# LSH attention and a mixture of causal heads: the second pair of heads without a scale, and one ring for q and k

## The chip, the cores and the metric

One core of a Trainium2 chip. The metric is the device time of one launch in microseconds; lower is better. TensorE (PE) does matmuls and transposes, VectorE (DVE), ScalarE (ACT) and GpSimd (POOL) elementwise work and reductions; in this kernel SyncE (SP) issues every DMA.

## The reference

Two stages, for 4 sequences (B) of 768 rows (S). The first is attention in 8 heads (H) of 64 columns (D) in which a query sees only the keys of its own bucket; the bucket is the sign pattern of 6 projections:

```python
q_bits = (einsum('bhsd,dk->bhsk', q, proj) > 0)          # same for k
mask = q_bucket[:, :, :, None] == k_bucket[:, :, None, :]
scores = where(mask, scale * q @ k.T, -1e9)               # scale = 1/8
x = softmax(scores) @ v                                   # heads side by side: (B, S, 512)
```

The second is a mixture of 4 causal heads (E) on x, of which a row takes the two with the largest gate logits:

```python
q, k, v = x @ wq[e], x @ wk[e], x @ wv[e]
ye = softmax(causal(scale * q @ k.T)) @ v @ wo[e]
out += (row chose e) * weight * ye
```

Inputs and output are 32-bit floats.

## The kernel before

**Units.** The work is cut into 48 units of attention: 32 of the first stage (`("L", b, h)`, written L0 to L7 here for the first sequence) and 16 of the second (`("M", b, e)`). `seq` is their order; the first sequence's L0 to L7 come first, later the mixture's units of sequence b − 1 stand between the heads of sequence b. Step i of the main loop is unit `seq[i]`. Heads are prepared in pairs (`hp`); the first pair is L0 and L1, the second L2 and L3, the third L4 and L5.

**One unit of the first stage.** Scores are made twice. `max_steps` (tile `mx`) makes them with queries on partitions, and DVE reduces their row maxima into `pm` (or `pmw` for a wide unit); `shift_steps` turns these into a row that is moved by DMA into the q operand (`qa<-row`, or `xth<-roww`). Then `s_unit` makes the transposed scores in 9 chunks of 512 (tile `st`, each from two products, `ka` with `qa` and `kb` with `qb`), ACT takes the exponential of each chunk twice (`p32` in four bytes, shown as p; `ph` in two), POOL makes the remainder `pl`, and PE multiplies with `vh` and `vl` into `o` (`av`). The maxima of `seq[i + 2]` are listed at step i. Bucket signs are extra rows of the operands, made in `signs`: `m0` on DVE, `M` (or `Mw`) on ACT, then four moves by DMA (`move`).

**Two widths.** A product of 32-bit precision is built from a rounded value and a remainder. Narrow operands are two-byte floats, and so that nothing leaves their range, q, k and v of a pair are scaled by powers of two from their largest absolute values: `pair_scales` reduces natq, natk and natv on DVE (tile `mqk`, 128x768) and goes through two matmuls' worth of transposes and some ten small DVE operations (`scale_of`) to `CS`. `prep_pair` then transposes q and k (PE), writes the scaled value (`qa`, `ka`) and the remainder (`qb`, `kb`), and projects for the signs with `pbh` and `pbl`, which `proj_halves` makes from proj. Wide operands are four-byte (`float32r`) and need no scale: `prep_first` does so for the first pair alone, in buffers of the names `xth` and `xtl` that later hold the mixture's input; it writes a plain copy as well (`T`), which the projection `pbd` reads in four bytes. Its v is scaled by itself in `prep_v`. Either way the halves of the operands lie on the wrong partitions at first and are moved by DMA (in the prep functions, and in `halves`).

**Buffers.** Narrow operands have four rings of `QB` = 5 buffers ("qa", "ka", "qb", "kb"), for units of both stages (`prep_pair`, `proj_steps`). A ring gives its buffers in the order in which they are asked for.

**Order.** All instructions are first recorded, each with the operations that it depends on. A `gate` adds a dependence that the data don't have (for example, the load of the second pair's q waits for the first pair's last remainder, `marks["t"]`, that of k for the signs, `marks["m"]`). `Recorder.schedule` then plans all engines with a cost for each operation: an engine takes what can start first, and among those what was recorded first. The plan sets the order of each engine's queue; on the chip each works through its queue in order. Background work is a list of jobs with a first and a last step (`job(first, last, generator, needs...)`). Until the first `av` PE runs placeholder matmuls (`o<-ident`) where it would be idle.

All operations are issued in one helper, so the profile shows line L423 for all of them; they are told apart by their tiles.

Of the kernel before, what the change touches and what calls it, by code (L numbers as in the profile page):

```python
# [429 lines left out]
LN_SHIFT = 5.545177444479562  # L430
EPS = 1e-9 * 256.0
LAG = 4
QB = 5
SCT = 4.0
FILL_GAP = 40.0
COLD = 4500.0
C0 = C1 = C2 = C3 = C4 = C5 = C6 = C7 = C8 = 0.0
FIRST = {("k", 1): "m", ("v", 1): "row", ("q", 2): "m", ("k", 2): "m"}
P1 = -3
YB = 2  # L440
NATB = 2
GS = "t"
W0 = 2
WN = 1
RATE = 750.0
# [4 lines left out]
def tile_kernel(ctx, tc, q, k, v, proj, w_gate, wq, wk, wv, wo, out):  # L450
# [20 lines left out]
    def raw(ap):  # L471
        return ap.bitcast(FT)
# [6 lines left out]

    def load(nm, src, b, hp):  # L480

        nc.gate = marks[FIRST.get((nm, hp), "m" if nm == "v" else "t") if not b else "m" if nm == "v" else "t"]
# [182 lines left out]

    def pair_scales(b, hp):

        second = (b, hp) == (0, 1)
        while second and "t" not in marks:
            yield 0  # L670
        m = sb.tile([128, 3], FT, name="mqk", bufs=2)
        names = "qk" if second else "qkv"
        for i, nm in enumerate(names):
            nc.gate = marks[GS] if second else None
            nc.vector.tensor_reduce(m[:, i:i + 1], NAT[nm, b, hp].rearrange("p h j d -> p (h j d)"), axis=AX.X, op=OP.max,
                                    apply_absolute_value=True)
            nc.gate = None
# [12 lines left out]
        yield 330  # L690
# [8 lines left out]
            a, n = (ds[g % 2]["qa"], MR) if g < 2 else (ds[g % 2]["ka"], MR + rows)  # L699
            move(a[D:D + n].rearrange("p (j s) -> p j s", j=2), M[32 * g:32 * g + 2 * n][:, None, :])  # L700

    def prep_first():

        ds = []
        lo, hi = slice(0, D), slice(D, 2 * D)
        ev, od = slice(0, HS), slice(HS, S)
        for h in range(2):
            d = U["L", 0, h] = dict(wide=True)
            d.update({n: sb.tile([128, S], FR, name=t, bufs=4) for n, t in
                      (("qa", "xth"), ("ka", "xtl"), ("qb", "xth"), ("kb", "xtl"))})  # L710
            ds.append(d)
        nats = {nm: NAT.pop((nm, 0, 0)) for nm in "qk"}
        TT = {nm: sb.tile([128, 2, HS], FT, name="T" + nm, bufs=1) for nm in "qk"}
        M = sb.tile([128, HS], FR, name="Mw", bufs=1)
        for nm, h in [("q", 0), ("k", 0), ("q", 1), ("k", 1)]:
            d, nat, T = ds[h], nats[nm], TT[nm]
            a, r = (d["qa"], d["qb"][:, od]) if nm == "q" else (d["ka"], d["kb"][:, ev])
            p = misc()
            for t in range(NT // 2):
                nc.tensor.transpose(p[:, t * 128:(t + 1) * 128],  # L720
                                    nat[:, h, 2 * t:2 * t + 2].rearrange("p j d -> p (j d)"), ident)
            nc.copy(T[:, h], p[:, :HS], bias=C0)
            nc.copy(a[:, ev], p[:, :HS], 0.125 if nm == "q" else None, bias=C0)
            if nm == "q":
                marks["t"] = nc.vector.scalar_tensor_tensor(r, p[:, :HS], 0.125, raw(a[:, ev]), op0=OP.mult,
                                                            op1=OP.subtract)
            else:
                marks["t"] = nc.vector.tensor_tensor(r, p[:, :HS], raw(a[:, ev]), op=OP.subtract)
            nc.sync.dma_start(raw(a[lo, od]), raw(a[hi, ev]))
            if nm == "k":  # L730
                p = misc()
                gs = (h, 2 + h)
                for g in gs:
                    nc.tensor.matmul(p[32 * g:32 * g + 32, :HS], pbd, TT["q" if g < 2 else "k"][:, h], start=True,
                                     stop=True, tile_position=(0, 32 * g))
                signs(p, gs, ds, [slice(32 * g, 32 * g + 32) for g in gs], M, 2, 1)
            yield 109 * (NT // 2)
        marks["m", 0, 0] = marks["m"]
        yield 700

    def proj_halves():
# [16 lines left out]
    def prep_pair(b, hp):  # L758
# [2 lines left out]
        lo, hi = slice(0, D), slice(D, 2 * D)  # L761
        ev, od = slice(0, HS), slice(HS, S)
        for h in range(2):
            d = U["L", b, 2 * hp + h] = {}
            d.update({n: sb.tile([128, S], HF, name=n, bufs=QB) for n in ("qa", "ka", "qb", "kb")})
            ds.append(d)
        nats = {nm: NAT.pop((nm, b, hp)) for nm in "qk"}
        c = SC.pop((b, hp))
        parts = []
# [359 lines left out]
        yield 0  # L1129

    def proj_steps(b, e):
        qa, ka, qb, kb = (sb.tile([128, S], HF, name=n, bufs=QB) for n in ("qa", "ka", "qb", "kb"))
        if b not in QKC:

            sc = QKC[b] = sb.tile([128, 4], FT, name="qkc")
# [128 lines left out]
    for b in range(B):  # L1264
        for hp in range(HP):
            i = pos["L", b, 2 * hp]
            if b or hp:
                loads.append((i - 4.5 if b or hp > 1 else P1, "q", q, b, hp))
                loads.append((i - 4.5 if b or hp > 1 else P1, "k", k, b, hp))
            loads.append((i - 4.5 if b or hp > 1 else P1 if not hp else -1, "v", v, b, hp))  # L1270
            job(max(i - 3.4, -1) if b or hp else -5, max(i - 2.6, -0.5) if b or hp else -4, prep_pair(b, hp) if b or hp else prep_first(),
                *([("sc", b, hp), "pb"] if b or hp else []))
            if not (b or hp):
                job(-1.3, -1, proj_halves())
            if b or hp:
# [142 lines left out]
```

## Time and profile before

| | |
|---|---|
| three timed runs | 671.19, 672.34, 673.12 us; median 672.34 |
| the profiled execution | 673.69 us, its span 671.9 us |
| mean granted TensorE clock | 0.996 |
| busy share of the span | PE 96%, PE weight loads 77%, DVE 76%, ACT 75%, POOL 70% |
| DMA | 50.02 MB, mean 74 GB/s |

The span is the time from the first to the last instruction. A busy PE is not PE at its peak: matmuls are pipelined, and their ends are modelled. What a stage is worth is read from that stage, so the rows below cut the span into stages.

### The profile page before, as it was taken

Reading aid. Unit: us, or ns where it says so; the run is one execution under the profiler, and the core shown is the slowest. Engines: PE = TensorE matmul, PEld = TensorE weight load, DVE = VectorE, ACT = ScalarE, POOL = GpSimd, SP = SyncE. Lnnn points to the kernel's source line nnn. Section 1 sums busy time; section 2 is a strip of 40 time slices with the busy share of each in tenths; the row PEclk is TensorE's granted clock in tenths of the full one; section 3 lists DMA queues with packets and bytes.
Section 4 is the critical chain, followed back from the end, with each engine's and each line's share of the span. In section 5 each row is a group of like instructions: output and inputs, shape, how many; then the busy total and the mean of one; then the engine's idle time right before and its main releaser. Section 6 shows DMA issues by size and latency. Waiting matters only on the chain.

```text
span 671.9 us, 21643 instructions
## 1 busy us (share of the span) xinstructions
PE 647.9 (96%) x8344; PEld 515.9 (77%) x8344; DVE 511.2 (76%) x1281; ACT 505.4 (75%) x1081; POOL 467.9 (70%) x496
## 2 busy tenths in 40 slices
PE   8998898999999999999999999899999999999997
PEld 7876666667887787888778777688778778789885
DVE  5969799898779786976975797886985867456652
ACT  3286888987887978876975879695995687953773
POOL 3186889887786968775883788584795596961652
PEclk9998999999999999999999999999999999999999
DMA  4642634444042334233132333323142221011222
GB/s 102 126 97 58 137 76 98 111 86 114 14 106 59 80 73 96 49 74 76 43 85 81 96 93 65 86 55 78 26 100 68 81 65 32 3 26 28 58 83 96
DMA packets 109933, 50.02 MB, mean 74 GB/s; under 512 B 88446, under 2 KB 106246, under 8 KB 109830
## 3 DMA queue, kind: packets, MB, share of 16 engines
q1 hardware_dynamic: 109830, 48.64, 30.7%
q8 instruction: 66, 1.08, 0.7%
q14 instruction: 37, 0.30, 0.2%
HBM read 20.98 MB, written 6.29 MB: 41 GB/s over the span
## 4 chain that ended last, share of the span: by engine, by line
PE 75%; DVE 11%; DMA 6%; ACT 3%; SPq 2%; issue 2%; POOL 1%; POOLq 0%; ACTq 0%; DVEq 0%
PE misc L423 27%; PE st L423 20%; PE o L423 19%; PE mx L423 10%; DVE pm L423 5%; DMA natv<-in_v_dram 3%; SPq L423 2%; ACT ph L423 1%; POOL pl L423 1%; ACT p L423 1%; DVE mqk L423 1%; DMA ka<-M 1%; DVE misc L423 1%; DMA qb<-qb 1%; DMA kb<-kb 1%
## 5 line engine op out<-in xcount | busy, mean ns | idle before, releaser
L423 POOL TENSOR_TENSOR pl<-p,ph 128x512 f16<-128x512 f32 (+2 forms) x384 | 423.9, 1130 | 184.6 <-ACT ph L423 107.3
L423 ACT ACTIVATE p<-st 128x512 f32<-128x512 f32 (+2 forms) x386 | 232.6, 603 | 52.3 <-PE st L423 49.8
L423 DVE TENSOR_REDUCE pm<-mx 128x2 f32<-128x512 f32 (+3 forms) x398 | 239.7, 621 | 30.6 <-PE mx L423 28.8
L423 ACT ACTIVATE ph<-st 128x512 f16<-128x512 f32 (+2 forms) x384 | 229.4, 602 | 1.2 <-PE o L423 1.2
L423 PEld LDWEIGHTS <-ph 128*128 128x128 f16 x2976 | 154.4, 98 | 24.7 <-issue 4.0
L423 PE MATMUL st<-qa,ka 78*128 78x512 f16 (+1 forms) x488 | 153.0, 323 | 3.0 <-ACT ph L423 1.6
L423 PE MATMUL st<-qb,kb 128*128 128x512 f16 x488 | 151.3, 321 | 0.0
L423 PEld LDWEIGHTS <-pl 128*128 128x128 f16 x1488 | 136.0, 97 | 9.3 <-POOL pl L423 4.3
L423 PE MATMUL mx<-ka,qa 76*128 76x512 f16 (+1 forms) x488 | 133.8, 322 | 5.1 <-DVE pm L423 2.4
L423 PE MATMUL o<-vh,pl 128*128 128x65 f16 x1152 | 126.1, 193 | 1.6 <-POOL pl L423 1.6
L423 PE MATMUL o<-vh,ph 128*128 128x65 f16 x1152 | 126.4, 194 | 0.7 <-DVE xp L423 0.2
L423 PE MATMUL o<-vl,ph 128*128 128x64 f16 x1152 | 126.1, 192 | 0.3 <-POOL vl L423 0.3
L423 PEld LDWEIGHTS <-qa 76*128 76x128 f16 (+1 forms) x488 | 44.9, 98 | 26.9 <-issue 9.3
L423 PEld LDWEIGHTS <-kb 128*128 128x128 f16 x488 | 48.1, 98 | 19.4 <-issue 5.2
L423 PEld LDWEIGHTS <-ka 78*128 78x128 f16 (+1 forms) x488 | 47.8, 98 | 14.7 <-issue 4.0
L423 PEld LDWEIGHTS <-ident 128*128 128x128 bf16 x469 | 36.7, 102 | 14.0 <-issue 4.8
L423 PE MATMUL o<-mvh,pl 128*128 128x65 f16 x336 | 35.8, 194 | 0.0
L423 PE MATMUL o<-mvh,ph 128*128 128x65 f16 x336 | 35.7, 194 | 0.0
L423 PE MATMUL o<-mvl,ph 128*128 128x64 f16 x336 | 35.7, 192 | 0.0
L423 PE MATMUL misc<-xth,wqk_h 128*128 128x384 f32 x128 | 32.1, 367 | 0.1
L423 DVE SCALAR_TENSOR_TENSOR kb<-misc,qkc,qa 128x384 f16<-128x384 f32 x32 | 19.6, 611 | 15.2 <-ACT qa L423 13.2
L423 POOL TENSOR_TENSOR vl<-cv,vh 128x384 f16<-128x384 f32 x32 | 28.2, 887 | 4.0 <-ACT vh L423 3.9
(204 smaller groups left out, 1126.5 us busy)
## 6 DMA issues: line engine op xcount, KB each, us to landing
natv<-in_v_dram SPq DMA_DIRECT2D x16, 384.0 KB
natq<-in_q_dram SPq DMA_DIRECT2D x15, 384.0 KB
natk<-in_k_dram SPq DMA_DIRECT2D x15, 384.0 KB
out_dram<-ot SPq DMA_DIRECT2D x20, 256.0 KB
qb<-qa SPq DMA_DIRECT2D x46, 96.0 KB
kb<-ka SPq DMA_DIRECT2D x46, 96.0 KB
ka<-qa SPq DMA_DIRECT2D x16, 96.0 KB
qb<-kb SPq DMA_DIRECT2D x16, 96.0 KB
```

The lines of the kernel that those rows point to most:

```text
L423: getattr(getattr(self.nc, e), m)(*[real(x) for x in args], **{k: real(x) for k, x in kw.items()})
```

## The change

The second pair of the first sequence is prepared as the first one: `prep_first` becomes `prep_wide(hp)`, for pairs 0 and 1.

- `pair_scales` is no longer called for the second pair: no mqk of q and k, no scale. Its preparation asks for the load of k and the end of the first pair's (`("pw", 0)`), not for the scale and the projection's halves.
- The load of its q is gated by nothing (`FIRST`), and the job runs from step −1.5 (`J1`), with a gate at the last projection of the pair before (`marks["p"]`).
- For the second pair the order is q, q, k, k, and the projections of both heads are made at the end, their signs with one operation on 128 partitions; its M moves have one row more per k (as the first pair's).
- q and k operands of both widths share one ring `qk` of `2 * QB` = 12 buffers of 3072 bytes: a wide operand takes one, a narrow head takes one for `qa` and `qb` together and one for `ka` and `kb`. So a wide pair takes eight, a narrow pair or two units of the mixture four. The wide first pair stays in `xth` and `xtl`; the mixture's transposed input, which its projections read, is in four bytes in these as before.

```diff
-QB = 5
+QB = 6
-FIRST = {("k", 1): "m", ("v", 1): "row", ("q", 2): "m", ("k", 2): "m"}
+FIRST = {("q", 1): None, ("k", 1): "m", ("v", 1): "row", ("q", 2): "m", ("k", 2): "m"}
-GS = "t"
+J1 = -1.5
...
-        second = (b, hp) == (0, 1)
-        while second and "t" not in marks:
-            yield 0
...
-        names = "qk" if second else "qkv"
+        names = "qkv"
...
-    def prep_first():
+    def prep_wide(hp):
...
         for h in range(2):
-            d = U["L", 0, h] = dict(wide=True)
-            d.update({n: sb.tile([128, S], FR, name=t, bufs=4) for n, t in
-                      (("qa", "xth"), ("ka", "xtl"), ("qb", "xth"), ("kb", "xtl"))})
-            ds.append(d)
-        nats = {nm: NAT.pop((nm, 0, 0)) for nm in "qk"}
+            ds.append(dict(wide=True))
+            U["L", 0, 2 * hp + h] = ds[h]
+        for n in "qk":
+            for d in ds:
+                for x in "ab":
+                    name = "qk" if hp else "xt" + ("h" if n == "q" else "l")
+                    d[n + x] = sb.tile([128, S], FR, name=name, bufs=2 * QB if hp else 4)
+        nats = {nm: NAT.pop((nm, 0, hp)) for nm in "qk"}
...
-        for nm, h in [("q", 0), ("k", 0), ("q", 1), ("k", 1)]:
+        for nm, h in [("q", 0), ("q", 1), ("k", 0), ("k", 1)] if hp else [("q", 0), ("k", 0), ("q", 1), ("k", 1)]:
...
+            nc.gate = marks["p"] if hp else None
             for t in range(NT // 2):
                 nc.tensor.transpose(...)
+            nc.gate = None
...
-            if nm == "k":
+            gs = () if nm == "q" else range(4) if hp and h else () if hp else (h, 2 + h)
+            if gs:
                 p = misc()
-                gs = (h, 2 + h)
                 for g in gs:
-                    nc.tensor.matmul(p[32 * g:32 * g + 32, :HS], pbd, TT["q" if g < 2 else "k"][:, h], start=True,
-                                     stop=True, tile_position=(0, 32 * g))
-                signs(p, gs, ds, [slice(32 * g, 32 * g + 32) for g in gs], M, 2, 1)
+                    marks["p"] = nc.tensor.matmul(p[32 * g:32 * g + 32, :HS], pbd, TT["q" if g < 2 else "k"][:, g % 2],
+                                                  start=True, stop=True, tile_position=(0, 32 * g))
+                signs(p, gs, ds, [slice(0, 128)] if hp else [slice(32 * g, 32 * g + 32) for g in gs], M, 2, 1)
...
-        marks["m", 0, 0] = marks["m"]
+        marks["m", 0, hp] = marks["m"]
+        done.add(("pw", hp))
...
     def prep_pair(b, hp):
-            d.update({n: sb.tile([128, S], HF, name=n, bufs=QB) for n in ("qa", "ka", "qb", "kb")})
+        for n in "qk":
+            for d in ds:
+                t = sb.tile([128, 2, S], HF, name="qk", bufs=2 * QB)
+                d[n + "a"], d[n + "b"] = t[:, 0], t[:, 1]
...
     def proj_steps(b, e):
-        qa, ka, qb, kb = (sb.tile([128, S], HF, name=n, bufs=QB) for n in ("qa", "ka", "qb", "kb"))
+        (qa, qb), (ka, kb) = ((t[:, 0], t[:, 1]) for t in (sb.tile([128, 2, S], HF, name="qk", bufs=2 * QB) for _ in range(2)))
...
-            job(max(i - 3.4, -1) if b or hp else -5, max(i - 2.6, -0.5) if b or hp else -4, prep_pair(b, hp) if b or hp else prep_first(),
-                *([("sc", b, hp), "pb"] if b or hp else []))
+            job(max(i - 3.4, -1) if b or hp > 1 else J1 if hp else -5, max(i - 2.6, -0.5) if b or hp > 1 else J1 + 0.5 if hp else -4, prep_pair(b, hp) if b or hp > 1 else prep_wide(hp),
+                *([("sc", b, hp), "pb"] if b or hp > 1 else [("ld", "k", 0, 1), ("pw", 0)] if hp else []))
...
-            if b or hp:
-                job(max(i - SCT, -2.6), max(i - SCT + 0.6, -0.6), pair_scales(b, hp), ("ld", "q", b, hp), ("ld", "k", b, hp),
-                    *([("ld", "v", b, hp)] if b or hp > 1 else []))
+            if b or hp > 1:
+                job(max(i - SCT, -2.6), max(i - SCT + 0.6, -0.6), pair_scales(b, hp), ("ld", "q", b, hp), ("ld", "k", b, hp), ("ld", "v", b, hp))
```

## Rows read from the trace of the kernel before

**Rows 1.** The page, busy time of the engines in us, their share of the span and their instructions, whole span.

```profile
PE 647.9 (96%) x8344; PEld 515.9 (77%) x8344; DVE 511.2 (76%) x1281; ACT 505.4 (75%) x1081; POOL 467.9 (70%) x496
```

**Rows 2.** Busy time by stretches of 28 us, two of the 24: the stretch, its length, then busy us and instructions of each engine, the granted TensorE clock, the DMA share and GB/s.

```profile
168.00:196.00 28.00, 27.78 (x393) 23.97 (x390) 20.12 (x58) 23.40 (x53) 21.77 (x22) 1.00 0.23 50
...
420.00:448.00 28.00, 26.15 (x345) 20.37 (x344) 25.51 (x61) 21.89 (x50) 19.26 (x20) 1.00 0.24 57
```

**Rows 3.** Busy time by the stages of the first 145 us, same columns as the group before.

```profile
16.00:28.00 12.00, 12.00 (x162) 10.64 (x160) 11.70 (x26) 0.00 (x0) 0.00 (x0) 1.00 0.66 138
28.00:36.00 8.00, 7.80 (x65) 6.43 (x62) 7.00 (x23) 6.93 (x16) 5.44 (x6) 1.00 0.60 132
36.00:46.00 10.00, 8.82 (x156) 6.90 (x156) 4.65 (x13) 8.54 (x18) 7.83 (x9) 1.00 0.10 25
46.00:60.00 14.00, 12.34 (x170) 9.07 (x171) 13.97 (x33) 10.64 (x24) 11.59 (x12) 0.98 0.65 129
60.00:63.00 3.00, 3.00 (x13) 2.07 (x12) 2.46 (x7) 0.74 (x2) 0.80 (x1) 0.50 0.00 0
63.00:76.00 13.00, 11.59 (x167) 8.62 (x166) 9.23 (x19) 10.81 (x24) 10.14 (x9) 1.00 0.44 92
76.00:92.00 16.00, 14.23 (x191) 10.23 (x189) 14.84 (x38) 13.25 (x28) 14.27 (x13) 1.00 0.40 96
92.00:119.00 27.00, 25.06 (x342) 18.26 (x341) 24.73 (x58) 23.82 (x50) 23.64 (x21) 1.00 0.44 98
119.00:145.00 26.00, 24.78 (x360) 18.00 (x359) 23.83 (x61) 23.25 (x52) 23.40 (x22) 1.00 0.40 92
```

**Rows 4.** Timeline of ACT (start us, duration us, engine, line, operation, out<-in, shapes, count, idle time before it and what ended it): the first and the last exponentials at the hand-over from one unit to the next, in order of time.

```profile
29.05 0.60 ACT L423 ACTIVATE p<-st 128x512 f32<-128x512 f32 x1 [13.38 <-PE st L423]
...
42.28 0.60 ACT L423 ACTIVATE p<-st 128x512 f32<-128x512 f32 x1 [1.12 <-PE st L423]
...
45.09 0.59 ACT L423 ACTIVATE p<-st 128x512 f32<-128x512 f32 x1
...
54.01 0.69 ACT L423 ACTIVATE ph<-st 128x512 f16<-128x512 f32 x1
...
62.84 0.60 ACT L423 ACTIVATE p<-st 128x512 f32<-128x512 f32 x1 [0.98 <-PE st L423]
...
101.62 0.57 ACT L423 ACTIVATE ph<-st 128x512 f16<-128x512 f32 x1
102.23 0.60 ACT L423 ACTIVATE p<-st 128x512 f32<-128x512 f32 x1
```

**Rows 5.** Timeline of DVE between 12 and 26 us, same columns: one remainder of the first pair, the row maxima of its first head and the reductions that stand between them.

```profile
12.16 0.56 DVE L423 SCALAR_TENSOR_TENSOR xth<-misc,xth 128x384 fp32r<-128x384 f32 x1
...
15.32 4.14 DVE L423 TENSOR_REDUCE pmw<-mx 128x2 f32<-128x512 f32 x6 [0.30 <-PE mx L423]
19.49 0.95 DVE L423 TENSOR_REDUCE mqk<-natq 128x1 f32<-128x768 f32 x1
...
24.39 0.94 DVE L423 TENSOR_REDUCE mqk<-natk 128x1 f32<-128x768 f32 x1
```

**Rows 6.** Timelines of PE, ACT, PE and DVE, same columns, a row each: steps of the second pair, in order of time, from a transpose of its k to the end of the row maxima of its first head.

```profile
35.25 0.50 PE L423 MATMUL misc<-ident,natk 128*128 128x128 f32 x3
...
40.55 0.62 ACT L423 ACTIVATE M<-m,sub_mul 128x384 f16<-128x384 f16 x1 [0.35 <-DVE m L423]
...
45.32 0.59 PE L423 MATMUL mx<-ka,qa 76*128 76x512 f16 x3
...
55.65 0.18 DVE L423 TENSOR_REDUCE negm<-pm 128x12 f32<-128x48 f32 x1
```

**Rows 7.** Timeline of SP (the DMA queue), same columns: loads and moves up to 46 us.

```profile
17.45 0.70 SPq L423 DMA_DIRECT2D natk<-in_k_dram  x1
...
25.54 0.77 SPq L423 DMA_DIRECT2D xth<-roww  x1
...
41.19 1.80 SPq L423 DMA_DIRECT2D qa<-M  x2
43.10 1.73 SPq L423 DMA_DIRECT2D ka<-M  x2
44.87 0.53 SPq L423 DMA_DIRECT2D natq<-in_q_dram  x1
```

**Rows 8.** Groups of DVE instructions by form between 28 and 84 us: out<-in, shapes, count, busy us, mean ns of one, idle time before and what ended it.

```profile
L423 DVE SCALAR_TENSOR_TENSOR kb<-misc,cs,ka 128x384 f16<-128x384 f32 x4 | 2.4, 614 | 0.5 <-ACT ka L423 0.5
...
L423 DVE TENSOR_SCALAR misc<-misc 128x1 int32<-128x1 int32 x3 | 0.5, 155 | 0.0
```

**Rows 9.** Groups of PE matmuls by form between 0 and 140 us, and of PE weight loads (PEld) between 20 and 140 us, same columns: narrow and wide scores.

```profile
L423 PE MATMUL st<-qa,ka 78*128 78x512 f16 x36 | 13.9, 387 | 1.8 <-ACT ph L423 1.1 <-DMA qa<-row 0.8
...
L423 PE MATMUL st<-qa,ka 78*128 78x256 f16 x36 | 9.4, 278 | 0.6 <-ACT ph L423 0.6
...
L423 PE MATMUL st<-xth,xtl 77*128 77x512 f32 x12 | 5.4, 447 | 0.3 <-ACT ph L423 0.3
...
L423 PE MATMUL st<-xth,xtl 77*128 77x256 f32 x12 | 3.6, 310 | 0.0
...
L423 PEld LDWEIGHTS <-kb 128*128 128x128 f16 x72 | 7.2, 100 | 4.2 <-issue 2.7
...
L423 PEld LDWEIGHTS st<-xth,xtl 77*128 77x128 f32 x24 | 4.6, 190 | 0.8 <-ACT ph L423 0.6
```

More of the change, by code (lines that the diff above doesn't have):

```diff
@@ L480, in load @@
     def load(nm, src, b, hp):
-        nc.gate = marks[FIRST.get((nm, hp), "m" if nm == "v" else "t") if not b else "m" if nm == "v" else "t"]
+        g = FIRST.get((nm, hp), "m" if nm == "v" else "t") if not b else "m" if nm == "v" else "t"
+        nc.gate = marks[g] if g else None
         t = sb.tile([128, 2, NT, D], FT, name="nat" + nm, bufs=NATB)
@@ L666, in pair_scales @@
     def pair_scales(b, hp):
-        second = (b, hp) == (0, 1)
-        while second and "t" not in marks:
-            yield 0
         m = sb.tile([128, 3], FT, name="mqk", bufs=2)
-        names = "qk" if second else "qkv"
+        names = "qkv"
         for i, nm in enumerate(names):
-            nc.gate = marks[GS] if second else None
             nc.vector.tensor_reduce(m[:, i:i + 1], NAT[nm, b, hp].rearrange("p h j d -> p (h j d)"), axis=AX.X, op=OP.max,
                                     apply_absolute_value=True)
-            nc.gate = None
             yield 0
@@ L724, in prep_first @@
             if nm == "q":
-                marks["t"] = nc.vector.scalar_tensor_tensor(r, p[:, :HS], 0.125, raw(a[:, ev]), op0=OP.mult,
-                                                            op1=OP.subtract)
-            else:
-                marks["t"] = nc.vector.tensor_tensor(r, p[:, :HS], raw(a[:, ev]), op=OP.subtract)
+                m = nc.vector.scalar_tensor_tensor(r, p[:, :HS], 0.125, raw(a[:, ev]), op0=OP.mult, op1=OP.subtract)
+            else:
+                m = nc.vector.tensor_tensor(r, p[:, :HS], raw(a[:, ev]), op=OP.subtract)
+            if not hp:
+                marks["t"] = m
             nc.sync.dma_start(raw(a[lo, od]), raw(a[hi, ev]))
-            if nm == "k":
+            gs = () if nm == "q" else range(4) if hp and h else () if hp else (h, 2 + h)
+            if gs:
                 p = misc()
-                gs = (h, 2 + h)
                 for g in gs:
-                    nc.tensor.matmul(p[32 * g:32 * g + 32, :HS], pbd, TT["q" if g < 2 else "k"][:, h], start=True,
-                                     stop=True, tile_position=(0, 32 * g))
-                signs(p, gs, ds, [slice(32 * g, 32 * g + 32) for g in gs], M, 2, 1)
+                    marks["p"] = nc.tensor.matmul(p[32 * g:32 * g + 32, :HS], pbd, TT["q" if g < 2 else "k"][:, g % 2],
+                                                  start=True, stop=True, tile_position=(0, 32 * g))
+                signs(p, gs, ds, [slice(0, 128)] if hp else [slice(32 * g, 32 * g + 32) for g in gs], M, 2, 1)
             yield 109 * (NT // 2)
-        marks["m", 0, 0] = marks["m"]
+        marks["m", 0, hp] = marks["m"]
+        done.add(("pw", hp))
         yield 700
@@ L763, in prep_pair @@
         for h in range(2):
-            d = U["L", b, 2 * hp + h] = {}
-            d.update({n: sb.tile([128, S], HF, name=n, bufs=QB) for n in ("qa", "ka", "qb", "kb")})
-            ds.append(d)
+            ds.append({})
+            U["L", b, 2 * hp + h] = ds[h]
+        for n in "qk":
+            for d in ds:
+                t = sb.tile([128, 2, S], HF, name="qk", bufs=2 * QB)
+                d[n + "a"], d[n + "b"] = t[:, 0], t[:, 1]
         nats = {nm: NAT.pop((nm, b, hp)) for nm in "qk"}
```

## The prediction

> **What bounds the kernel now.** I read the page first, then busy time in equal stretches, then the first 145 us by stages, and only then single timelines of the stages that the change touches. On the page TensorE (PE) is busy 647.9 of 671.9 us, the other engines 70 to 76% [rows 1]. The stretches divide this in two. Between 168 and 196 us PE is idle for 28 − 27.78 = 0.22 us, and 1.85 us in the worst stretch of the long middle [rows 2]: whatever starts earlier ahead of it lets the end come earlier by as much, and nothing else in it can be won. Before 145 us it is otherwise: from 92 to 145 us PE is busy 25.06 + 24.78 of 53 us (94%), and from 28 to 92 us 57.8 of 64, of which three microseconds (60 to 63) ran at a granted clock of 0.50, the lower of its two levels (1.2 GHz), after a stage in which PE was busy 12.34 of 14 us; in full-clock work that is 56.3 of 64 us (88%) [rows 3]. So the stretch up to 92 us is where time lies, and this is also where the second pair (heads 2 and 3, units L2 and L3) is prepared and first used.
>
> The exponentials on ACT show the hand-overs [rows 4]. A good one costs next to nothing: L4's last exponential ends at 101.62 + 0.57 = 102.19 and L5's first starts at 102.23. L1 ends at 54.70 and L2 starts at 62.84: a hole of 8.1 us. L0 runs from 29.05 and its ninth chunk comes only at 42.28, after ACT waited 1.12 us for PE; L1 starts at 45.09. Why L2 is late is read backwards [rows 6]: its row maxima end on DVE at 55.65 and begin behind the first mx matmuls at 45.32, and those wait for the sign rows, whose moves SP issues from 41.19 to 44.83 [rows 7]; the signs (M) are made at 40.55, from transposes that PE did up to 35.75 and on.
>
> **Part 1: second pair without a scale.** Its q and k need no maximum, so mqk, the scale chain behind it and the wait for the projection's halves go.
>
> (a) Start of L0. The two mqk reductions take 0.95 and 0.94 us on DVE, the first between the row maxima of L0 and the second in front of its row [rows 5]. Both go: −1.9. In their place DVE gets remainders of q, 0.56 each, if they are ready before the row maxima, which the early load of q allows: + 2 × 0.56. Sum −0.8. Bounds: −1.9 if they fall in a pause, and +1.8 if all four remainders (2.2), the sign operation (0.6) and one or two of the copies (0.9, at the price of a remainder each) get in ahead: 3.7 − 1.9. I take −0.8, nearest to the rows.
>
> (b) L0's own step. Three operations of ACT of the second pair (0.62 each by the one shown, 1.9 together [rows 6]) and PE's four groups of transposes (0.50 each, 2.0) leave the stretch 31 to 41 us, where L0's exponentials and its ninth chunk wait. I take −1.5 for L1's start: between 0 and 1.9 + 1.12 = 3.0, and by the single wait of 1.12 nearer the middle.
>
> (c) The hole. k's load is issued at 17.45 [rows 7] and mqk reads it at 24.39 without a wait for it, so it had landed. From the transposes of k to the first mx the narrow way took 45.32 − 35.25 = 10.1 us; with two more copies (T) of 0.56 that is 24.4 + 10.1 + 1.1 = 35.6, not 45.3. Even at the pace of before (45.32 to 55.65 for the maxima, then 7.2 to the first exponential) L2 could start at 53.1; DVE, busy 4.65 of 10 us between 36 and 46 [rows 3], leaves room to be quicker. L1 would end at 54.7 − 0.8 − 1.5 = 52.4. So the hole closes nearly: L2 some 10 us earlier.
>
> (d) What is given back. The hole is one of exponentials, not of work: DVE is busy 13.97 of 14 us between 46 and 60 [rows 3]. So I ask how early L4 can start (the 92 us mark) if 28 to 92 is filled as well as 92 to 145 was, engine by engine, with L0's start at 0.8 earlier. Before 28 us PE's 12 us were placeholders and maxima alone, and ACT and POOL were idle, so the preparation moved there costs them nothing.
> DVE: 52.2 us of work, less seven operations of the pair at 0.61 and ten small ones at 0.155 [rows 8], 5.8, plus what its k work pushes past 28 (two remainders and the signs, 1.7, less the mqk of 0.94): 0.8. That is 47.1. At the 91.6% of 92 to 145 this takes 51.5 us: L4 at 78.7.
> ACT: 50.9 − 1.9 = 49.0, at 88.8% 55.2 us, and 1.0 until its first exponential: 83.4.
> POOL: 50.1, at 88.8% 56.4 us, and 2.3 until its first chunk (two exponentials of 0.60 after the first's start): 85.9, which is −6.1.
> PE: 56.3 − 2.0 for the transposes + 1.5 for wide weights (next part) = 55.8, at 94.0% 59.3 us: 86.5, which is −5.5.
> The last of these sets it: −5.5, not the 10 of the chain. From L4 on the work is that of before, and the end comes 5.5 earlier.
>
> **Part 2: four-byte operands.** L2 and L3 have 36 matmuls each (24 st, 12 mx), half of 512 columns, half of 256. The wide ones of the first pair show means of 447 against 387 ns and 310 against 278 [rows 9], so at most 36 × 0.060 + 36 × 0.032 = 3.3 us for both units; the means hold waits, so the lower end is 0; I take 1.5, the middle. The loads of weights go from 100 to 190 ns. The Trainium skill (TensorE: Matmul & The Clock Gate, section Weight-path perf modes) says that the fast weight load is not used for FP32 weights, and the trace agrees (190 against 100 ns); by that rule the time would be the fourth rival's. The pair's moves between partitions double in bytes; the DMA engines' share of 0.10 between 36 and 46 us [rows 3] is their cover; without it each waits for the next load, and L2 has 10 us in hand against that.
>
> **Part 3: one ring.** Twelve buffers of 3072 bytes, two for a unit, eight for the wide pair. Six units instead of five: no later stage waits longer for a buffer, so 0 in the middle. Only the fourth pair's k takes the buffers of L3's q, so its k waits for L3's last scores. The cover is that before, its k was copied after L3's end as well; without it L6 loses what the early preparation gains. At the best it removes idle time like the 1.85 us of one stretch [rows 2]; I take 0. The loads for the third pair hang on the second pair's signs; from 44.87 they move up by about the same 10 us as the signs.
>
> **Sum.** The profiled execution took 673.69 us (671.9 of span and 1.8 around it): −5.5 gives 668.2. The median of the three timed runs is 1.35 lower, so I forecast 666.8. Its own range: wide weights 0 or 3.3 (−1.6 or +1.9 at 94%), L0's start −1.1 or +2.6 beside what was taken: together 664.1 to 671.3.
>
> **Rivals.**
> 1. The hole moves to L4. For: DVE is full while it lasts, and L4 was itself late by DVE (14.84 of 16 us before 92). Against: DVE has 10 us in 28 to 46 and 63 to 76 unused. If the third pair's chain does not move, L4 starts where it did: 672.3, or 673.8 if PE's clock falls once more as at 60 to 63 (1.5 us).
> 2. L0 starts late. The second pair's operations stand in front of L0's row on DVE (11.70 of 12 us busy between 16 and 28), and its four sign moves (3.6 us on SP) in front of the row's move at 25.54: +1.8 + 3.6 = 5.4 instead of −0.8, so 6.2 worse: 673.0, and 676 if half of the hole's gain is lost with it. It decides from a first exponential 4.7 us late (29.05 + 4.7 = 33.8). For: the preparation is listed among L0's maxima. Against: q lands early and k's work comes after L0's maxima.
> 3. More than forecast: the holes before L4, L6 and the next sequence close too, and 92 to 145 us fills to 98% instead of 94: 53 × 0.04 = 2.1 and a quick start (1.1 + 1.6): 662.
> 4. Weight loads show in full. Each of the 72 takes 0.09 more: 6.5 us, against 1.5 taken; (6.5 − 1.5) / 0.94 = 5.3: 672.1. Against: 256 more columns cost 0.109 us (387 − 278), so 512 columns cover a load of 0.190.
>
> **How the numbers follow.** Forecast 0.55, rival 1 0.16, rival 2 0.12, rival 3 0.10, rival 4 0.07. A change of 0.3%, 2.0 us, is about what a measurement of this kernel can tell from none. Faster is the forecast, rival 3, 0.02 of rival 1 and 0.03 of rival 4: 0.70. Same is 0.10 of rival 1, 0.04 of rival 4 and 0.04 of rival 2: 0.18. Slower is the rest of rivals 1 and 2: 0.12. The range takes in half of rival 3 below and rivals 1 and 4 above and leaves out the worse part of rival 2: 661.0 to 673.5.
>
> **What would show it.** (a) first exponential of L0 at 28.2; later than 30, the step is wrong. (b) L1's first near 42.8. (c) mx of L2 before 37 and L2's first exponential within 1 us of L1's last; no stretch of granted clock 0.5 between 50 and 70 us. (d) the start of L4 near 86.8; if it is 92, the gain was given back, if below 84, PE and POOL were filled better than after 92. Part 2: PE's busy time per unit of L2 and L3 up by under 1.7 us. Part 3: idle time of PE after 168 us as before. What would make the prediction wrong most simply is a new order of all queues in the middle, since the planner sets all of them anew: the idle time per 28 us would show it.

## The result, and the profile after

| | kernel before | with the change |
|---|---|---|
| median of the timed runs, us | 672.62 (671.19 to 674.58) | 678.13 (675.62 to 679.55) |
| profiled execution, us | 673.69 | 677.74 |
| its span, us | 671.9 | 676.0 |

The ratio is 1.0078, with a 95% interval of 1.0051 to 1.0104: slower by 0.8%. The forecast was 666.8, 0.8% faster, with 0.12 on slower. The busy line of the page answers [rows 1]:

```profile
PE 647.3 (96%) x8326; PEld 517.7 (77%) x8326; DVE 506.1 (75%) x1262; ACT 510.0 (75%) x1092; POOL 468.2 (69%) x496
```

PE's work did not grow (647.3 against 647.9 us), so the 4.1 us of span are waiting. Where they come in is read from the same exponentials in both traces. First the timeline of ACT after the change: the first exponential of L0, of L1 and of L2 (p), then that of L4, of the third sequence's first head and of the mixture's first unit of the third sequence (ph). The first three answer [rows 4].

```profile
30.60 0.60 ACT L423 ACTIVATE p<-st 128x512 f32<-128x512 f32 x1 [1.49 <-PE st L423]
...
44.50 0.63 ACT L423 ACTIVATE p<-st 128x512 f32<-128x512 f32 x1
...
60.04 0.60 ACT L423 ACTIVATE p<-st 128x512 f32<-128x512 f32 x1
...
87.39 0.60 ACT L423 ACTIVATE ph<-st 128x512 f16<-128x512 f32 x1
...
284.20 0.67 ACT L423 ACTIVATE ph<-st 128x512 f16<-128x512 f32 x1
...
515.14 0.59 ACT L423 ACTIVATE ph<-st 128x512 f16<-128x512 f32 x1
```

The last three in the kernel before:

```profile
92.78 0.60 ACT L423 ACTIVATE ph<-st 128x512 f16<-128x512 f32 x1
...
284.50 0.64 ACT L423 ACTIVATE ph<-st 128x512 f16<-128x512 f32 x1
...
510.82 0.59 ACT L423 ACTIVATE ph<-st 128x512 f16<-128x512 f32 x1
```

L0 starts 1.6 us late, L2 2.8 us early, L4 5.4 us early. That lead is gone at 284 us (0.3), and at 511 us the kernel is 4.3 us behind (3.5 one unit later, 3.6 at the last exponential, 4.1 by the spans). So there are two losses behind L4: 5.1 us before 284 and some 4 to 4.6 between 284 and 511. One execution of each kernel was profiled, and the timed ones of one kernel spread over several us, so a lead of 1 or 2 us between two profiles can be chance. Busy time by stages after the change, same columns as [rows 3] (the last two stages have no row there):

```profile
16.00:28.00 12.00, 11.99 (x151) 10.37 (x148) 11.58 (x22) 0.87 (x2) 0.00 (x0) 1.00 0.66 135
28.00:36.00 8.00, 6.61 (x55) 4.74 (x53) 5.96 (x19) 6.24 (x15) 3.95 (x5) 1.00 0.68 156
36.00:46.00 10.00, 8.58 (x131) 7.29 (x128) 5.21 (x12) 9.58 (x21) 9.75 (x10) 1.00 0.57 115
46.00:60.00 14.00, 13.95 (x205) 11.96 (x205) 12.86 (x34) 11.14 (x24) 11.72 (x12) 1.00 0.54 110
60.00:63.00 3.00, 3.00 (x35) 2.32 (x34) 3.00 (x8) 3.00 (x8) 1.97 (x3) 1.00 0.41 93
...
284.00:520.00 236.00, 229.78 (x2980) 184.18 (x2979) 180.28 (x450) 183.25 (x397) 166.21 (x159) 0.99 0.31 72
...
435.20:437.00 1.80, 1.64 (x8) 1.00 (x9) 1.80 (x5) 0.94 (x3) 0.91 (x1) 0.50 0.01 2
```

and the same long stage before:

```profile
284.00:520.00 236.00, 232.58 (x3033) 187.03 (x3032) 185.31 (x461) 185.35 (x401) 168.85 (x162) 1.00 0.31 73
```

There is no half clock at 60 to 63 us (1.00), as forecast; but PE is busy 2.8 us less between 284 and 520, and there the granted clock falls to its lower level (0.50 from 435.2 to 438.6) after PE stood still. Half of these 3.4 us, 1.7, is my estimate of what the fall costs; 2.8 + 1.7 = 4.5 is the size of the second loss.

What PE waits for in that stage (engine, tile waited with, releaser: us in total, times, longest), after the change in the first two rows and in the kernel before in the third; the kernel before has no row for pm at all:

```profile
PE mx L423 <- DVE pm L423: 4.4, 4, 1.9
PE mx L423 <- DVE mqk L423: 0.8, 1, 0.8
...
PE misc L423 <- DVE row L423: 2.1, 2, 1.6
```

What DVE itself waits for with mqk there, after the change (before: 3.6, 1.9 and 0.3 for natv, natk and natq):

```profile
DVE mqk L423 <- DMA natv<-in_v_dram: 5.3, 5, 2.3
DVE mqk L423 <- DMA natk<-in_k_dram: 1.7, 3, 0.7
DVE mqk L423 <- DMA natq<-in_q_dram: 1.1, 1, 1.1
```

The longest of these waits, in the timelines of SP, DVE and PE after the change:

```profile
421.27 6.96 SPq L423 DMA_DIRECT2D qk<-qk  x11
428.27 0.59 SPq L423 DMA_DIRECT2D natv<-in_v_dram  x1
```

```profile
433.51 0.95 DVE L423 TENSOR_REDUCE mqk<-natv 128x1 f32<-128x768 f32 x1 [2.31 <-DMA natv<-in_v_dram]
...
434.64 0.67 DVE L423 TENSOR_REDUCE pm<-mx 128x2 f32<-128x512 f32 x1
```

```profile
433.18 0.33 PE L423 MATMUL st<-qk 67*128 67x384 f16 x1
435.36 0.61 PE L423 MATMUL mx<-qk 76*128 76x512 f16 x1 [1.86 <-DVE pm L423]
```

DVE's queue goes in order, and at its head stands the maximum of a v that is still on its way: issued at 428.27 behind eleven moves, it can be read at 433.51, 5.2 us later. DVE idles 2.31 us; the row maxima (pm) stand behind, and PE's mx waits 1.86 us for a buffer that they should free. The kernel before meets a v that has not landed at the same place, and PE waits 1.6 us there, for the row:

```profile
433.28 0.95 DVE L423 TENSOR_REDUCE mqk<-natv 128x1 f32<-128x768 f32 x1 [1.62 <-DMA natv<-in_v_dram]
```

So this longest wait shows the mechanism and is not the difference. The difference is in the other four of the change (pm 2.5 us in all, mqk 0.8), each behind a maximum that waited 0.4 to 0.8 us for its load, where the kernel before has one of 0.5 us.

So the first theory: **the change gives the middle another order, and in that order DVE's maxima of loads that have not landed hold PE more often.** The rivals: the ring of buffers itself holds something longer; the four-byte pair costs it; or a new order is a matter of luck.

### The profile page after: what moved, and what is told of

Its sections match the earlier page's. It is cut to its first block, busy times and chain, and to the rows that moved or that the text cites. A ratio compares the mean times of both kernels' runs of the same rounds, so it can differ in the third digit from the quotient of the medians.

```text
span 676.0 us, 21606 instructions
## 1 busy us (share of the span) xinstructions
PE 647.3 (96%) x8326; PEld 517.7 (77%) x8326; DVE 506.1 (75%) x1262; ACT 510.0 (75%) x1092; POOL 468.2 (69%) x496
## 4 chain that ended last, share of the span: by engine, by line
PE 66%; DVE 11%; DMA 10%; ACT 6%; issue 3%; SPq 2%; POOL 1%; ACTq 0%; POOLq 0%; DVEq 0%
PE misc L423 25%; PE st L423 17%; PE o L423 14%; PE mx L423 9%; DMA natv<-in_v_dram 5%; DVE pm L423 4%; ACT ph L423 2%; ACT p L423 2%; SPq L423 2%; DMA natk<-in_k_dram 1%; DVE mqk L423 1%; DVE qk L423 1%; DMA qk<-M 1%; DVE xtl L423 1%; DMA ot<-in_moe_wk_dram 1%
## 5 line engine op out<-in xcount | busy, mean ns | idle before, releaser
L423 ACT ACTIVATE p<-st 128x512 f32<-128x512 f32 (+2 forms) x386 | 230.2, 598 | 35.9 <-PE st L423 32.2
L423 DVE TENSOR_REDUCE pm<-mx 128x2 f32<-128x512 f32 (+2 forms) x380 | 228.3, 619 | 36.7 <-PE mx L423 35.4
L423 PE MATMUL st<-qk 78*128 78x512 f16 (+2 forms) x976 | 226.7, 324 | 2.4 <-ACT ph L423 1.1
L423 PEld LDWEIGHTS <-qk 78*128 78x128 f16 (+4 forms) x1392 | 122.7, 98 | 63.0 <-issue 18.1
L423 PE MATMUL mx<-qk 76*128 76x512 f16 (+2 forms) x488 | 133.5, 324 | 8.5 <-DVE pm L423 6.1
L423 PE MATMUL o<-vl,ph 128*128 128x64 f16 x1152 | 123.6, 192 | 0.7 <-POOL vl L423 0.7
L423 ACT ACTIVATE qk<-misc,qkc 128x384 f16<-128x384 f32 x27 | 15.7, 581 | 26.0 <-PE misc L423 26.0
L423 DVE SCALAR_TENSOR_TENSOR qk<-misc,cs,qk 128x384 f16<-128x384 f32 x56 | 33.3, 606 | 0.8 <-ACT qk L423 0.7
L423 DVE SCALAR_TENSOR_TENSOR qk<-misc,qkc,qk 128x384 f16<-128x384 f32 x32 | 19.6, 612 | 15.8 <-ACT qk L423 13.7
L423 PE MATMUL misc<-xth,wqk_l 128*128 128x384 f32 x128 | 30.9, 360 | 0.0
L423 POOL TENSOR_TENSOR vl<-cv,vh 128x384 f16<-128x384 f32 x32 | 28.2, 888 | 2.3 <-ACT vh L423 2.3
```

What stands on the lines that cost most here:

```text
L423: getattr(getattr(self.nc, e), m)(*[real(x) for x in args], **{k: real(x) for k, x in kw.items()})
```

## Experiments

All ratios are to the kernel before, timed on the same chip beside it, with 95% intervals. "Ahead at L4" is against 92.78 in the rows above.

### Ring, depth, order, load

**e1_ring**: the one ring alone, in the kernel before.

```diff
-QB = 5
+QB = 6
...
-            d.update({n: sb.tile([128, S], HF, name=n, bufs=QB) for n in ("qa", "ka", "qb", "kb")})
...
+                t = sb.tile([128, 2, S], HF, name="qk", bufs=2 * QB)
+                d[n + "a"], d[n + "b"] = t[:, 0], t[:, 1]
...
```

> The kernel before with the ring alone: one ring of 12 buffers for q and k, the second pair narrow and with its scale as before. Ring theory (operands that share a ring get their buffers at the wrong time, and the middle waits): the first 145 us as before, then 5 to 9 us lost, in all +4 to +8 us on 672.6. Order theory (every edit makes the planner put all queues in another order, and it is that order that loses): no fixed sign, the start as before, the total anywhere within 5 us of before. Wide theory (the four-byte second pair itself brings the loss): 0 within 1 us.

Measured: 676.92 us, ratio 1.0062 (1.0034 to 1.0091). The ring alone costs most of what the change costs, with no four-byte pair in it. Between 284 and 520 us PE waits as it does after the change (there 4.4):

```profile
PE mx L423 <- DVE pm L423: 4.1, 4, 1.6
```

But most of its loss falls earlier: in its profile it is 1.1 us behind at L4, 4.5 at the third sequence's first head and 5.0 at the last exponential. So these waits alone are not what sets it back; which wait does so before 284 us stays open.

**e3_depth**: six buffers in four rings (`QB = 6`, nothing else).

> The kernel before with four rings of 6 buffers instead of 5 and nothing else. Ring theory (the sharing is at fault, not the depth): 0 within 1 us. Order theory: the deeper rings let the planner start preparations earlier, so the order changes; up to 5 us in either direction. Wide theory: 0 within 1 us.

Measured: 672.58, 0.9989 (0.9966 to 1.0012). The depth does nothing that can be measured.

**h4_order**: the kernel with the change; from L4's first scores on, the planner's order is replaced by a list with the order and the engines of the kernel before.

```diff
-        return order
...
+        return [x for x in order if x[0].i not in own] + [(self.ops[i], self.ops[i].alts[j]) for i, j in late]
```

> The changed kernel, with the operations that the kernel before issues from the first scores of L4 on put in the order (and on the engines) of the kernel before; all before that in the changed kernel's own order. No operation is left out or added. Order theory: the 5.4 us that L4 has gained stay to the end, 667 +- 1.5 us, and idle time of PE from 168 to 590 us as in the kernel before. Ring and wide theories: the same operands with the same buffers wait as they did in the changed kernel, 676 to 679 us.

Measured: 672.15, 0.9979 (0.9958 to 0.9999), 1.0% under the change with the same operations and buffers, though not the 667 that was expected. In its profile it is ahead by 3.7 us at L4 (not 5.4; the list reaches into the preparation of the third pair, which I take for the cause) and by 4.1 at 511 us: nothing is lost there.

**h_ring**: e1_ring, with the whole order of the kernel before, placeholders included (the same edit, for all operations).

> The kernel before with the one ring of 12 buffers (as in e1_ring), and every engine's queue in exactly the order of the kernel before, placeholders included. Order theory (the ring costs nothing by its buffers; it only makes the planner choose another order): as the kernel before, ratio 0.997 to 1.003, and PE's waits for row maxima (pm) between 168 and 590 us near the 0.5 us of before instead of the 4.1 of e1_ring. Ring theory (q's value and remainder in one buffer are held longer, or a buffer is given later): as e1_ring, ratio 1.006.

Measured: 673.98, 0.9994 (0.9971 to 1.0016); no row for pm among PE's waits from 284 to 520. So the ring by itself costs nothing: with the old order it runs as the old buffers do. What costs is the order that the planner gives it. That theory is settled by this run and h4_order together.

**e4_load**: the change, but the second pair's q is loaded behind the first pair's last remainder, as before.

```diff
-FIRST = {("q", 1): None, ("k", 1): "m", ("v", 1): "row", ("q", 2): "m", ("k", 2): "m"}
+FIRST = {("k", 1): "m", ("v", 1): "row", ("q", 2): "m", ("k", 2): "m"}
```

> The changed kernel, but the second pair's q is loaded after the first pair's last remainder, as before, and not ungated. Meant for L0, whose first exponential came at 30.6 us instead of 29.05. If q's four operations on DVE and its move ahead of L0's maxima and moves cause that, L0 starts at 29 us or earlier, and L2 keeps its gain; if the moves of k cause it, L0 stays at 30.6. The total: order theory, anywhere from 668 to 680, as the middle is planned anew; ring and wide theories, 676 to 678.

Measured: 669.35, 0.9923 (0.9894 to 0.9951): faster than both kernels, by one gate. It is 10.1 us ahead at L4. Busy time from 28 to 92 us, e4_load, and the placeholders in it:

```profile
28.00:92.00 64.00, 63.04 (x888) 51.66 (x881) 56.30 (x133) 58.59 (x123) 57.18 (x54) 1.00 0.53 112
...
L423 PE MATMUL o<-ident 128*128 128x128 bf16 x68 | 4.5, 219 | 0.0
```

PE is busy 63.04 of 64 us, but placeholders are 3.1 of these by the trace (their 4.5 overlap with other matmuls); without them it is 60.0, or 94%. What the early q does shows in the timelines of SP, DVE and PE, in order of time. After the change:

```profile
18.81 1.71 SPq L423 DMA_DIRECT2D qk<-qk  x1
20.56 0.59 SPq L423 DMA_DIRECT2D xth<-xth  x1
...
25.31 0.46 SPq L423 DMA_DIRECT2D xth<-xth  x1
...
25.36 0.27 DVE L423 TENSOR_SCALAR roww<-misc 6x128 fp32r<-6x128 f32 x1
...
26.50 0.78 SPq L423 DMA_DIRECT2D xth<-roww  x1
...
29.83 0.73 PE L423 MATMUL st<-xth,xtl 77*128 77x512 f32 x2 [1.40 <-DMA xth<-roww]
...
33.54 0.62 DVE L423 TENSOR_SCALAR m<-misc,sub_mul 128x384 f16<-128x384 f32 x1 [0.23 <-PE misc L423]
```

and e4_load, with its first exponential (ACT):

```profile
17.37 1.66 SPq L423 DMA_DIRECT2D xth<-xth  x1
...
22.37 0.46 SPq L423 DMA_DIRECT2D xth<-xth  x1
...
23.01 0.27 DVE L423 TENSOR_SCALAR roww<-misc 6x128 fp32r<-6x128 f32 x1
...
23.31 0.77 SPq L423 DMA_DIRECT2D xth<-roww  x1
...
26.52 0.75 PE L423 MATMUL st<-xth,xtl 77*128 77x512 f32 x3
...
28.67 0.62 DVE L423 TENSOR_SCALAR m<-misc,sub_mul 128x384 f16<-128x384 f32 x1
...
30.69 1.07 PE L423 MATMUL st<-xth,xtl 128*128 128x512 f32 x5
31.20 0.60 ACT L423 ACTIVATE p<-st 128x512 f32<-128x512 f32 x1 [1.26 <-PE st L423]
```

After the change q's own moves go ahead of the halves of L0 on SP: these start at 20.56 instead of 18.20 (by SP's timeline before), their second hop waits for the landing of the first until 25.31, and the row's move stands behind it to 26.50, though the row had been ready since 25.63. On DVE q's two copies and two remainders (2.2 us) stand ahead of L0's row maxima. Without this the row is ready 2.4 us sooner and the scores start 3.3 us sooner. L0 does not gain by it: the second product of its first chunk comes only at 30.69, and its first exponential at 31.20, later than the change's 30.60 and far from the 29 that was expected. What comes earlier is the second pair. Its signs (m) are made at 28.67 instead of 33.54, as their projections no longer stand on PE behind scores that wait for the row; its sign moves start at 29.97 instead of 37.20, and the mx of L2 at 34.86 instead of 41.35.

**h_e4**: e4_load, with the order of before from L4's first scores on.

> The kernel with the change and the second pair's q loaded behind the first pair's last remainder (e4_load), with the operations from L4's first scores on in the order of the kernel before. Order theory: the 10.1 us that e4_load has won at L4 stay to the end instead of 8.0 in its profile, so a span near 662 and a ratio 0.003 or more below that of e4_load (0.992): 0.985 to 0.990. Capacity theory (what is early in L4 is lost behind it in any order, since the engines are full): as e4_load, 0.992, with PE's waits moved to other places.

Measured: 671.17, 0.9957 (0.9928 to 0.9985), no better than e4_load. A miss: only 7.0 us are ahead at L4 (the cut falls into the preparation of the third pair, which I take for the cause), of which 4.9 are left at 372 us and 1.2 at 458. The old order is not good for every program. The result by itself fits the capacity theory as well; e8_best below, which keeps its lead, speaks against that.

### The loads in DVE's queue

**e5_land**: the change; the planner alone takes each load of q, k and v to land 1.5 us later, so it places mqk later.

```diff
-                end += 900.0
+                end += 900.0 + (1500.0 if o.outs and o.outs[0].tile.name in ('natq', 'natk', 'natv') and o.i > 1000 else 0.0)
```

> The kernel with the change; the planner alone is told that the loads of q, k and v land 1.5 us later than it took them to (first pair left out), so that it places their maxima (mqk) later in DVE's queue. Queue theory (mqk stands at the head of DVE's in-order queue for a load that has not landed, the row maxima wait behind it, and PE's mx behind those): DVE's waits for natq, natk and natv fall well under the 12 us of the change, PE's waits for pm between 168 and 590 us from 4.4 to under 2, and the time to 671 to 675. Rival (the waits for loads only stand where DVE had nothing to do): 677 to 679, as the change.

Measured: 675.41, 1.0019 (0.999 to 1.0049), just above the 671 to 675 expected. The part in question goes as the theory has it: PE's waits for pm between 168 and 590 us fall from 4.4 to 1.3. But the new plan changes earlier stages too: it is 5.4 us ahead at L7 and 1.2 behind at the second sequence's second head; in between PE's clock is at 0.50 from 143.0 to 146.4.

**e6_both**: the same on e4_load.

> e4_load (q behind the first pair's last remainder) with the planner's landing 1.5 us later as in e5_land. Queue theory: 2 to 4 us below e4_load, ratio 0.986 to 0.990. Rival: as e4_load, 0.992.

Measured: 669.44, 0.99 (0.9856 to 0.9943), as e4_load; 10.9 us ahead at L6 and 1.4 at L7, where PE stood 3.6 us for a remainder of the next pair and then ran at a clock of 0.50 from 116.5 to 123.3. The profile is of the slowest of its six executions (671.11; the least is 664.91).

**e7_late**: the change with the later landing for the third and fourth sequence alone; up to their loads the plan is that of the change. `load` sets a flag on these DMAs, and the planner reads it.

```diff
+        if b > 1:
+            op.bias = 0
...
-                end += 900.0
+                end += 900.0 if o.bias else 2400.0
```

> The kernel with the change; the planner is told that the loads land 1.5 us later for the third and fourth sequence alone, so the plan is that of the change until these are loaded (e5_land moved the first stages as well and lost 6 us between 129 and 158 us). Queue theory: up to M(0,1) as the change (1.75 us ahead of before), then PE idle between 284 and 520 us near 7 us as in e5_land instead of 14, so an end 1 to 4 us ahead of before: ratio 0.995 to 1.000. Lottery theory (each new order is good or bad by chance, the waits for loads have no special part): anywhere between 0.995 and 1.010.

Measured: 672.7, 0.9968 (0.9948 to 0.9987): 1.1% under the change. Busy time from 284 to 520 us, and all that DVE waits for with mqk there:

```profile
284.00:520.00 236.00, 234.89 (x3019) 187.55 (x3017) 183.82 (x465) 186.85 (x406) 167.55 (x161) 1.00 0.33 77
```

```profile
DVE mqk L423 <- DMA natv<-in_v_dram: 0.2, 1, 0.2
```

The waits for pm have no row any more, and PE's 229.78 us are 234.89. (So PE's idle time falls from 6.2 to 1.1 us; the 14 and 7 of the expectation are not what these windows show.) The kernel is 0.7 us ahead at the third sequence's first head and 3.2 at the last exponential, where the change goes from 0.3 ahead to 3.6 behind: the second loss goes with DVE's waits for loads. That they are all of it isn't shown. The change's fall of the clock (1.7 us by the estimate above) is missing here too, and e4_load, whose profile has as long waits for pm in this stage (4.1 us) and no such fall, goes from 9.1 to 7.9 us ahead.

**e8_best**: e4_load with the same later landing.

> e4_load with the later landing of e7_late. Queue theory: the 9 to 11 us that e4_load is ahead at L(1,7) stay, a span near 662 and a ratio of 0.986 to 0.990 against 0.992 of e4_load. Lottery theory: 0.988 to 1.000.

Measured: 663.69 (661.61 to 665.63), 0.983 (0.98 to 0.986): the fastest of all, 1.7% under the kernel before. Its lead of 8.8 us at L4 is 8.6 at 284 us and 9.9 at the last exponential. Its busy line and its long stage:

```profile
PE 644.9 (97%) x8355; PEld 516.5 (78%) x8355; DVE 504.4 (76%) x1263; ACT 510.4 (77%) x1091; POOL 468.0 (71%) x496
```

```profile
284.00:520.00 236.00, 233.21 (x2992) 185.90 (x2993) 182.18 (x463) 184.26 (x402) 164.55 (x159) 1.00 0.33 77
```

**g1_before_late** and **g2_ring_late**: the same later landing in the kernel before, and in e1_ring.

> The kernel before, with the planner told that the loads of the third and fourth sequence land 1.5 us later. PE waits only 0.5 us for row maxima between 168 and 590 us there, so if the later landing mends the ring's harm alone: 0.997 to 1.001. If it helps any kernel: as much as from the change to e7_late, 0.990 to 0.993.

> e1_ring (one ring, nothing else changed) with the same later landings. Queue theory: what e1_ring lost between 284 and 520 us comes back, 1.000 to 1.003 instead of 1.006, and then e7_late and e8_best are below it by what the four-byte pair wins early (0.4 to 0.8% and 1.2 to 2%). Rival (the ring's order loses elsewhere as well): as e1_ring, 1.006.

Measured: 671.19, 0.9964 (0.9942 to 0.9987), and 672.0, 0.9994 (0.9974 to 1.0014). So the later landing gives the kernel before 0.4%, e1_ring 0.7%, e4_load 0.9% and the change 1.1%. It is partly a gain that was there in any case, and mends more where the ring's order had done harm. With it in place the four-byte pair is worth 0.3% with the early load (e7_late against g2_ring_late) and 1.6% without (e8_best). Against the kernel before with the same landing (g1_before_late) the change as it is gains nothing (0.9968 against 0.9964), and e8_best 1.3%.

### How much of it is luck

**n1_wait** and **n2_land**: the kernel before with one constant of the planner moved by a hair.

```diff
-WAIT = 75.0
+WAIT = 77.0
```

```diff
-                end += 900.0
+                end += 910.0
```

> The kernel before; nothing but one constant of the planner is moved by a hair (an assumed wait of 75 ns becomes 77), which gives other orders of the queues with the same work, buffers and dependences. Measures what a new order alone is worth. Queue theory in its narrow form: within 0.3% of before as long as no load is read earlier. Lottery theory: off by some tenths of a per cent in either direction, and by the same places (PE's waits for pm behind mqk).

> The kernel before with another hair: the assumed landing of each DMA 910 instead of 900 ns. As n1_wait: 0.997 to 1.003 if an order is worth little by itself, 0.99 to 1.01 if the order of the middle is a lottery.

Measured: 0.9993 (0.997 to 1.0016) and 0.9995 (0.9974 to 1.0016). Such a change of the order costs nothing. Two draws are few, and they moved the plan by little; the next two show that another plan can cost 0.7 or 0.9%. So whether the ring's order is worse by a trait of the ring or by a bad draw stays open.

**g3_late1** and **g4_best1**: e7_late and e8_best with the later landing for the second sequence too, for the first loss (L7 to 284 us), which e7_late leaves (5.5 us ahead at L4, 0.7 at the third sequence's first head).

> e7_late with the later landing for the second sequence's loads as well. Queue theory for the first part too: 3 to 5 us ahead of before at L(2,0) instead of 0.7, and a ratio of 0.990 to 0.994 instead of 0.997. Another trait of the order: 0.995 to 1.000, with the loss between L7 and L(2,0) as large as before.

> e8_best with the same. It loses nothing between L4 and L(2,0) as it is (8.8 and 8.6 us ahead), so under the queue theory 0.981 to 0.985, as e8_best.

Measured: 1.0034 (1.0009 to 1.006) and 0.9919 (0.9888 to 0.9951), both worse than without (a part of g3_late1's is the clock: its executions have a median of 0.994, those of e7_late 0.999). In g3_late1 the lead is gone by the second sequence's first head (4.5 us at L7, −0.2 there), although DVE's waits for v and k between 92 and 284 us fall from 5.0 to 0.9. So the first loss is not the loads'. It belongs to the order of that stretch as well, since h4_order with the same operations keeps its lead there; which wait in it decides stays open: PE's rows there are many and small (the largest 1.3 us). Nor is a later landing a gain wherever it is put.

## Why the prediction was wrong, step by step

**What bounds the kernel.** Right: PE is full behind 168 us, and only waits can be won or lost. But from "whatever starts earlier ahead of it lets the end come earlier by as much" I went on as if the middle would stay as it was. Where PE is idle 0.22 us in 28, there is little to win and all to lose (e7_late shows how little: 1.1 us idle between 284 and 520, against 3.4 before).

**(a) L0's start**, −0.8 to 28.2: wrong, 30.60. All of q's four operations got ahead on DVE (its row is 0.1 us later than before). The rest I had not costed: the row's move is issued 1.0 us later than before (26.50 against 25.54), behind q's moves and L0's halves on SP, and the scores start 1.8 us later (29.83 against 28.07). I counted the moves of the signs there, as rival 2, but not those of q, which the ungated load brings forward. Without the early load the part on DVE held (the row is ready at 23.01 instead of 25.25), and the step still failed: the first exponential comes at 31.20, after the second product of its chunk.

**(b) L1 near 42.8**: 44.50, 0.6 us earlier than before instead of 2.3; it started late with L0.

**(c) The hole**: mx of L2 before 37 was forecast; they come at 41.35, and L2 starts at 60.04, 5.2 us behind the end of L1. In e4_load mx come at 34.86 and L2 starts at 56.93. The chain was read rightly, but its start hung on what was early in the queues. There is no half clock between 50 and 70 us, as expected; that the change did this isn't shown. In n1_wait, n2_land and e3_depth PE is busy 12.4 to 12.5 of the 14 us from 46 to 60, about as before (12.34), and 60 to 63 us run at 1.00 too; in h_ring, with 12.44, at 0.50.

**(d) L4 5.5 us earlier**: 5.39, right as a number and by chance. Two of its terms were off against each other. By the trace, without placeholders, PE had 54.0 us of work in the 59.4 us up to L4 (27.2 to 86.6 us, by the mark of the prediction), 91%; the forecast was 55.8 in 59.3, 94%. So there was 1.8 us less to do, and PE was filled less, by the late start under (a). As a fill the 94% can be had: e4_load has 51.2 us of work in 54.7. "From L4 on the work is that of before, and the end comes 5.5 earlier" is the step that failed: the work was that of before, the order was not.

**Part 2, four bytes.** Groups of PE matmuls by form up to 140 us after the change, wide and narrow, against [rows 9]:

```profile
L423 PE MATMUL st<-qk 77*128 77x512 f32 x12 | 5.5, 457 | 0.1
...
L423 PE MATMUL st<-qk 128*128 128x512 f32 x12 | 5.0, 417 | 0.0
...
L423 PE MATMUL st<-qk 78*128 78x512 f16 x24 | 9.1, 379 | 0.6 <-ACT ph L423 0.3 <-DMA qk<-row 0.2
...
L423 PEld LDWEIGHTS st<-qk 128*128 128x128 f32 x24 | 4.6, 192 | 0.3
```

437 ns on the mean against 379 is the 0.06 us that I took as the upper end, and the load of weights takes 192 ns as in [rows 9]. The same comparison over all 72 four-byte matmuls of L2 and L3 gives 3.3 us, so the 1.5 taken was too small by up to 1.8 (the means hold waits). Rival 4, in which the loads show in full, did not come: it asks for 6.5. The rule on fast weight loads (the Trainium skill, TensorE: Matmul & The Clock Gate, section Weight-path perf modes) holds here by the 192 ns, but had no price of its own.

**Part 3, the ring at 0**: the step that cost most. As a buffer it is 0 (h_ring, 0.9994). But one ring instead of four changes when the planner finds a buffer free, so it changes each queue behind it, and that order costs 0.6% (e1_ring). My argument, "no later stage waits longer for a buffer, so 0", answers another question than the one that the time asks.

**Rivals and chances.** None of the four is what happened. Rival 2 had the place (the row's move behind the second pair's on SP) and not the operations, and at 30.60 it was far from the 33.8 from which it should decide. The new order of the middle stands in the last sentence of my text as the simplest way to be wrong, without a chance or a price; as a rival with both it would have put more than 0.12 on slower.

## What to carry to other kernels

Where a program plans its own queues, a change of buffers is a change of all orders: cost it in two steps, once with the old order kept and once with the new one, and ask where an in-order queue has at its head something that comes by DMA. When such an operation waits, look at what stands behind it and who waits for that; here DVE's 2.3 us became PE's 1.9. And an early load is not free for being early: it brings its copies and moves forward too, into queues that other work needs sooner. And before an engine is called full, its placeholders are to be taken off: 63 busy us of 64 were 60 of work.

## What was not expected of the hardware

A load of 384 KB could be read 5.2 us after its issue (428.27 to 433.51), where the planner takes some 4.4 (1.28 + 2.18 + 0.9); telling it 1.5 us more, in the right place, turned a kernel 0.8% slower into one 0.3% faster (and the kernel before into one 0.4% faster). And the granted clock fell to 0.50 (1.2 GHz) behind one pause of PE of 1.86 us, where it had been at 1.00 before; e7_late, without that pause, has 1.00 over 284 to 520. The same pause doesn't always bring a fall: behind 1.8 us the clock falls in n2_land, behind 1.7 in e4_load and 2.1 in n1_wait it stays.

So executions of one kernel differ by their clock. Four of e4_load's eleven have a mean granted clock of 0.999 or 1.0 and take 665.0 to 666.9 us; the other seven have 0.994 to 0.997 and take 669.3 to 671.2. All six of e8_best have at least 0.999. Of the 5.7 us between the medians of the two, 2.3 are left between executions at such a clock, so more than half of e8_best's gain over e4_load goes with the clock. The runs don't show whether its order prevents the falls or the six were lucky.
